# A new order of the jobs of a fused attention and MLP kernel behind its first 85 jobs, with a new table of PSUM banks

## The chip, the cores and the metric

The kernel runs on one core of a Trainium2 chip. The metric is the device time of one execution in microseconds (us); the comparison uses the median of several runs. Engine names in rows: PE is TensorE (PEld its weight loads), DVE is VectorE, ACT is ScalarE, POOL is GpSimd, SP is SyncE, which issues nearly all DMAs (SPq is its queue).

## The reference

One input of 2048 tokens by 512 features is normalised. From it two branches are computed and added to the input:

```
xn = layernorm(x)
# branch A: 32 heads of 16, four segments of 512 tokens
q, k, v = xn @ wq, xn @ wk, xn @ wv
for s in range(4):
    logits = q_s @ k_s.T * scale + mask          # causal inside the segment
    a_dot  = softmax(logits) @ v_s
    a_mem  = phi(q_s) @ M / (phi(q_s) @ z + 1e-6) # memory of the earlier segments
    o_s    = g * a_mem + (1 - g) * a_dot
    M, z   = M + phi(k_s).T @ v_s, z + sum(phi(k_s))
A = o @ wo
# branch B: MLP on layernorm(xn), 512 -> 1792 -> 512
B = gelu(layernorm(xn) @ w1 + b1) @ w2 + b2
out = x + A + B
```

## The kernel before

The work is cut into 1307 jobs, each a short run of instructions on one or more engines. Attention runs in 16 units `i` (segment times group of eight heads), the MLP in 16 half blocks `j` (256 tokens times half of the 1792 hidden features). The kernel keeps high and low halves of its numbers in f16, so that a dense product takes three matmuls for one.

Jobs are named by tuples. Those of which the texts speak:

- `T i,1` and `T i,0`: keys and queries of unit i (line 480, 12 matmuls of 512 columns); then ScalarE (514, 517) and VectorE (518, 529, 530) take the bank, and SP writes the halves to DRAM and reads them back.
- `M i,n` (621, 628): twelve score jobs that find the maximum of every row. `R i` (499, 638, 639, DMAs 641 and 644): the maxima are turned by TensorE, split by ScalarE and VectorE, written to DRAM (`md<-mhl`) and read back as two more rows of the queries (`qst<-md`).
- `S i,t,n` (661, 666, 675): the scores again, with these rows, then ScalarE's exponential and GpSimd's mask. `S i,0,0` is the first that reads the rows of `R i`.
- `pv`/`PV` (690, 698, 699, 703, 704): probabilities times values. `O i,0` to `O i,2` (714, 540, 541, 545, 546, 720, 722, 725, 726): division by the sum of the row, on all engines but TensorE.
- `Z`, `Qd`, `Q` (560, 571, 576, 577, 583): the part that reads the memory.
- `D j,f` (480 with 256 columns, 756), `G j` (763), `H j,c` (770, 771, 772): hidden features, GELU, halves; `e j,n` (797): the second MLP product, six matmuls a job.
- `out s,b` (815): the output projection of 128 tokens.

Each engine does its instructions in the order in which the jobs are recorded. Nothing but the string `ORDER` sets this: each letter takes the next job of one stream (a for the norm, f and g for `T`, i for `M` and `R`, j for `S`, k for `pv`, l for `O`, m for `Z`, `Qd`, `Q` and `K`, o for `D`, p for `G` and `H`, q for `e`, r for `out`, s for the accumulators, the rest for weights). Each PSUM tile takes the bank that the next digit of `BANKS` names, of eight (`ps0` to `ps7`); a matmul that starts a tile waits until the last reader of the bank's tile before is done. Semaphores for all waits are derived from the order.

Of the kernel before, what the change touches and what calls it, by code (L numbers as in the profile page):

```python
# [56 lines left out]
def streams():  # L57
# [42 lines left out]


ORDER = (
    "aatcucuccvavtctveecttcetcuvaactvuvtaatcattavdtubcwwvccfwxxcxwxyxyxxgyhxcoxxvwxofooowcvwzyzoiyyiazgyyziiynzoiiys"
    "ppAnziiniicvzvcniiooAzmAihiiopzqqiqcivpqjpqjijqqijizqjiqqjiiAwszBzoAskkkkmjiAojoijsoAijAqjqjasAfoAopgkkkkpjpjqq"
    "jlpoolojjjooilihAAkkkkpaiqqiqijqjqqijqjiqjqjisBfgpiiqkkkkmpliqqiooiqpBlqoBopohijjiojiijpolsjiqaqajqiqiqqiiqapka"
    "kmkktspaqijqiqjqiqajqbqajopijjgBfopkkkBkjjjlooooBlhjjjolqiqqiipkkkkjiqqijqqjjiqiqjjqiqiqiBkkkkmpliilfnplimpngrr"
    "mrjjponijqjqjinjipiskmkkmkaiijrijjoojiqsjqqjiqiiiqqkkkkihlqlfmlogojqjqjqqjjasoojmkkkkmqjiqjqjjaojjpipmooisikkkk"
    "lpilhiofmgoooqiqpppqiqiqqqiiiqqpsosmoiqqiiqiqppsslooijqjojijojijoiaakkkkmpaijqjqjaqqqjiqqjiqjqiikmkkakbqiaqqahl"
    "olfqjjojqmjgjjoolmmkkkkmhjjoojjiitjiojiippkkkkliiilnfnimpligniinipmrrijjrsijqjqiqjiqjqiipkmkkksiqjqijqjqjiqjqii"
    "qjqikmpkkkiprlqsphlfojmjgopjjlojpjoomokmkkkqiqisjojiqisjqiqijqqijqhiqqiiqjsqiiqppmkkkkilalofomqpgopaoooospmlajq"  # L110
    "qqjqqjqjqiiqiqqqjqiqqipipooooiijooppoiaakkkkmajiqpisqqjiqjqjaiqaqhjqqqjqaaqmkkkkbjlfoljqjmjgojjqolmkkkkmmjjjooj"
    "jioijoiiippkpkkkiinliifniiilnnimlgrpmjjrmjjjrrijikkpskkiqqijqiqijqqjiqjiqjqiqjiqiispqkpkskksqilqoplfojmjgjjjpoo"
    "oojolmkkkkiqjiqpsjiqiqijqjqiqijqjiqiqiqiiqqkksmkpikplolfjjqmjgjjjoooooklpkmkkjiiopjqiqijqjiqpjqiqijqiqqiqiiqikk"
    "pspkkqiplpoooopljjjqqqjqjjqooolkpskmkpkmqqqpqjpjqqqjqjqpqqjqjqqqkmkkkqlllqqqqqqqqqrrrr"
)

BANKS = (
    "012345670123457063571265407321640573216405732164053271640527163054271630542713605427105472105427105472105472015"  # L120
    "470251407251405712470512470512470536124075631254076340125637123756123576132576132576132576132576135402761350427"
    "163054273106542736574326574326537425632754632574631072456310724563071245360712453620731620731067203617621073621"
    "073621073621037621037621037261702361475023671540263701524603175246031746013746013713460713471630471630463714067"
    "314056723410523674105236741052367410527410527410527410527410527140352671450326475103264751023674523674523647253"
    "647236547236475264735264107532410765324107265431067512043675120436751204736152047361520473615270346150312750317"
    "250317253107250371257013275027135027134650132754062751340621375460376054370567403056374065374065307645307645307"
    "642153076241076241076241076253410762534621075346210754316024310264310432610432610324610324612403246013752640163"
    "754207156437120564371205647312056473120564731206547321065473265104723607423460273460273642073642073642051736420"
    "157642031765420316750316705315631705630157630157630157306173504621357462017345620147536210436024136024316403216"
    "403216403216403216740536740536740536740536271406"  # L130
)


# [777 lines left out]
```

## Time and profile before

| | |
|---|---|
| three runs | 694.29, 694.91, 697.16 us, median 694.91 |
| profiled execution | span 693.1 us; its own time beyond the span is not given |
| TensorE matmuls | 678.7 us busy, 98% of the span, 6359 instructions |
| VectorE | 535.4 us, 77% |
| ScalarE | 522.7 us, 75% |
| GpSimd | 347.2 us, 50% |
| TensorE clock | granted share 0.83 between 20 and 40 us, 1.00 in every other stretch of 20 us |

The span goes from the first to the last instruction of the program; the 1.8 us up to the median lie outside it. Matmuls overlap each other, so a TensorE that is shown busy may still have lost time between two of them: what it lost is read from the starts of its instructions and from the waits of its weight loads.

### The profile page before, as it was taken

How to read it: one execution, taken by the hardware profiler on the slowest of the kernel's cores; microseconds unless marked ns; L12 is line 12 of the kernel's file. 1: busy time of each engine (PE TensorE's matmuls, PEld its weight loads, DVE VectorE, ACT ScalarE, POOL GpSimd, SP SyncE). 2: the span in 40 equal slices, each digit the busy share in tenths (PEclk: the TensorE clock that was granted, in tenths of full speed). 3: DMA queues.
4: the chain of work that ended last, by engine and by line, in shares of the span. 5: the costliest groups of instructions: out<-in, count | busy, mean ns of one | idle time of the engine just before them, and what ended most of it. 6: DMA issues, size and time to landing. Idle time of an engine off the chain costs nothing.

```text
span 693.1 us, 16949 instructions
## 1 busy us (share of the span) xinstructions
PE 678.7 (98%) x6359; PEld 395.7 (57%) x6359; DVE 535.4 (77%) x1695; ACT 522.7 (75%) x1013; POOL 347.2 (50%) x533
## 2 busy tenths in 40 slices
PE   7799999999999999999999999999999999999997
PEld 6465556576654555566554456567564456656653
DVE  4499978897795887998798786888678595969442
ACT  5989898878795659857795697757795687778870
POOL 5276768365624425664334445454362546455752
PEclk9899999999999999999999999999999999999999
DMA  9984222420204213431113224231120416140101
GB/s 272 283 238 136 64 63 63 108 62 14 84 10 115 87 44 74 100 71 33 51 45 92 63 72 99 63 93 33 31 80 24 132 18 152 18 108 3 18 1 61
DMA packets 51790, 55.12 MB, mean 80 GB/s; under 512 B 4782, under 2 KB 40636, under 8 KB 51708
## 3 DMA queue, kind: packets, MB, share of 16 engines
q1 hardware_dynamic: 49404, 49.84, 25.3%
q0 software_dynamic: 2304, 4.20, 3.7%
q8 instruction: 50, 0.82, 0.5%
q14 instruction: 32, 0.26, 0.1%
HBM read 36.99 MB, written 17.04 MB: 78 GB/s over the span
## 4 chain that ended last, share of the span: by engine, by line
PE 78%; ACT 10%; POOL 4%; DVE 3%; issue 2%; DMA 1%; SPq 1%; POOLq 0%; ACTq 0%; DVEq 0%
PE ps L480 33%; PE ps L797 16%; PE ps L690 10%; PE ps L815 6%; PE ps L661 5%; PE ps L621 5%; ACT pt L666 2%; DVE ps L628 2%; PE ps L571 2%; PE ps L499 1%; ACT hT L763 1%; ACT hT L771 1%; SPq L252 1%; POOL w1s L371 1%; DMA pt<-in_A_wk_dram 1%
## 5 line engine op out<-in xcount | busy, mean ns | idle before, releaser
L628 DVE CUSTOM_DVE_ANT_0 ps<-ps,mask 128x512 f32<-128x512 f32 (+3 forms) x512 | 233.8, 522 | 16.1 <-PE ps L621 14.9
L666 ACT ACTIVATE pt<-ps,qkcs 128x512 f32<-128x512 f32 (+1 forms) x384 | 206.1, 624 | 35.3 <-PE ps L661 33.5
L797 PE MATMUL ps<-w2s,hT 64*128 64x512 f16 x1344 | 176.7, 376 | 0.2
L480 PE MATMUL ps<-xnT,w1s 128*128 128x256 f16 x1344 | 157.8, 273 | 0.0
L675 POOL TENSOR_SCALAR_AFFINE_SELECT pt<-pt 128x256 f32<-128x256 f32 x256 | 99.1, 414 | 92.0 <-ACT pt L666 91.0
L480 PEld LDWEIGHTS <-w1s 128*128 128x128 f16 x1344 | 127.3, 98 | 29.1 <-issue 11.3
L772 POOL TENSOR_TENSOR hT<-hh,hT 128x512 f16<-128x512 f32 x64 | 67.8, 1059 | 82.8 <-ACT hT L771 81.0
L797 PEld LDWEIGHTS <-hT 64*128 64x128 f16 x1344 | 76.3, 94 | 50.7 <-issue 6.0
L690 PE MATMUL ps<-pt,vt 128*32 128x512 f32 (+3 forms) x1024 | 77.3, 435 | 0.1
L756 DVE SCALAR_TENSOR_TENSOR hT<-ps,sc,sr 128x256 f32<-128x256 f32 x112 | 52.1, 478 | 27.2 <-PE ps L480 27.0
L628 DVE DVE_READ_ACCUMULATOR2_ANT mc<- 128x1 f32 x512 | 70.6, 138 | 0.0
L661 PE MATMUL ps<-qst,kst 50*128 50x512 f16 (+3 forms) x512 | 67.5, 298 | 0.3 <-ACT pt L666 0.2
L621 PE MATMUL ps<-kst,qst 48*128 48x256 f16 (+3 forms) x512 | 67.1, 297 | 0.5
L771 ACT ACTIVATE hT<-hh 128x512 f16<-128x512 f32 x64 | 36.6, 572 | 33.4 <-POOL hh L770 32.9
L690 PEld LDWEIGHTS ps<-pt,vt 128*32 128x32 f32 x1024 | 31.3, 109 | 42.4 <-issue 30.8
L770 POOL TENSOR_SCALAR hh<-hT,sc 128x512 f32<-128x512 f32 x64 | 41.8, 653 | 26.6 <-ACT hT L763 24.9
L720 POOL TENSOR_TENSOR nN<-nN,oT 128x512 f32<-128x512 f32 x16 | 20.3, 1267 | 61.3 <-DVE oT L546 61.3
L763 ACT ACTIVATE hT<-hT,b1t 128x256 f32<-128x256 f32 x112 | 46.4, 495 | 0.2
L480 PE MATMUL ps<-xnT,wqs 128*128 128x512 f16 x192 | 45.6, 389 | 0.0
L480 PE MATMUL ps<-xnT,wks 128*128 128x512 f16 x192 | 44.3, 379 | 0.0
L480 PE MATMUL ps<-wvs,xnT 128*128 128x512 f16 x192 | 44.0, 380 | 0.1
L815 PE MATMUL ps<-wos,oT 128*128 128x512 f16 x192 | 43.2, 380 | 0.6 <-POOL oT L726 0.6
(217 smaller groups left out, 890.0 us busy)
## 6 DMA issues: line engine op xcount, KB each, us to landing
kd<-hl SPq DMA_DIRECT2D x48, 128.0 KB
qd<-hl SPq DMA_DIRECT2D x48, 128.0 KB
kst<-kd SPq DMA_DIRECT2D x32, 192.0 KB
qst<-qd SPq DMA_DIRECT2D x32, 192.0 KB
acc<-in_A_x_dram SPq DMA_DIRECT2D x16, 256.0 KB
acc<-in_B_b_dram POOLq DMA_DIRECT2D x16, 256.0 KB, 4.1
out_dram<-acc SPq DMA_DIRECT2D x16, 256.0 KB
xt<-in_A_x_dram SPq DMA_DIRECT2D x14, 256.0 KB
```

Of the source, the lines that this page charges most:

```text
L480: T.matmul(p, wsl(ws, k, a), xsl(xs, k, b), start=s0 and i == 0, stop=s1 and i == 3 * n - 1)
L621: T.matmul(p[:, o:o + n], stk[i, 0][r, t, P * qb:P * qb + P], stk[i, 1][r, t, :n], start=True, stop=True)
L628: V.tensor_tensor_reduce(p[:, o:o + n], p[:, o:o + n], mask[:, 512 - n:], 1.0, -3e38, OP.add, OP.max, mc[:, 16 * b + 4 * t + qb:16 * b + 4 ...
L661: T.matmul(p[:, o:o + n], stk[i, 1][r, t, P * kb:P * kb + P], stk[i, 0][r, t, P * kb:], start=True, stop=True)
L666: A.activation(e[:, OFF[kbs[0]]:OFF[kbs[0]] + o], p[:, :o], AF.Exp, scale=qkcs[:, 1, i % NG:i % NG + 1])
L675: G.affine_select(v, v, pattern=[[0, 2], [1, P]], compare_op=OP.is_ge, fill=0.0, base=0, channel_multiplier=-1)
L690: T.matmul(p[32 * c:32 * c + 32, P * kb:], vt[s, kb][:, 4 * g + c, 16 * odd:16 * odd + 32], pt[i, 2 * c + odd][:, OFF[kb]:OFF[kb] + LEN[kb ...
L756: V.scalar_tensor_tensor(hz[:, fi, :], p[:, :256], col(F1 + fh), srow[hs][:, own], op0=OP.mult, op1=OP.mult)
L763: A.activation(z, z, AF.Gelu_apprx_tanh, bias=b1t[:, FH * (j % 2) + f:FH * (j % 2) + f + 1])
L772: G.tensor_tensor(hT[:, z, 1, :], t, hT[:, z, 0, :], op=OP.subtract)
L797: w = T.matmul(pes[j][a], hTs[fh][r, fi, u, P * a:P * a + P], w2s[r, fo, v, :], start=n == 0 and m == 0, stop=fi == FH - 1 and m == 2, ski ...
L815: T.matmul(p, o[:, u, P * b:P * b + P], wos[:, g, v, :], start=i == 0, stop=i == 3 * NG - 1)
```

## The change

The two strings are replaced. The first 85 letters of `ORDER` stay; behind them the same number of every letter stands in a new order, so every stream's jobs keep their order among themselves and no instruction is added or dropped. `BANKS` is a new list of the same length. The diff, cut to the first lines and the last two of each table:

```diff
 ORDER = (
-    "aatcucuccvavtctveecttcetcuvaactvuvtaatcattavdtubcwwvccfwxxcxwxyxyxxgyhxcoxxvwxofooowcvwzyzoiyyiazgyyziiynzoiiys"
+    "aatcucuccvavtctveecttcetcuvaactvuvtaatcattavdtubcwwvccfwxxcxwxyxyxxgyhxcoxxvwxofooowcswooyzyiiizvzyyzgiyvyizypz"
...
-    "pspkkqiplpoooopljjjqqqjqjjqooolkpskmkpkmqqqpqjpjqqqjqjqpqqjqjqqqkmkkkqlllqqqqqqqqqrrrr"
+    "pikkkkqiplmoooplqjjojqjjqjoolkokppkkqmqqqpjpqqqjjqqqqjpjqqjqqqqkmkkkqlqqqllqqqqqqqrrrr"
 )
 BANKS = (
-    "012345670123457063571265407321640573216405732164053271640527163054271630542713605427105472105427105472105472015"
+    "012345670123457063571265407321640266457031264537052164326705164327105264317035126473056473506437506437540463750"
...
-    "403216403216403216740536740536740536740536271406"
+    "327536427543627543672545036172450175240175264256"
 )
```

**GpSimd at `O 12,1`.** Lines 770 and 772 are `H 12` (halves of the hidden features), 720 and 722 are `O 12,1`, 675 is a mask of `S`, 780 adds the bias to an accumulator. Before:

```order
L780 DMA acc<-in_B_b_dram 128x512
L770 TENSOR_SCALAR hh<-hT_115,sc 128x512
L772 TENSOR_TENSOR hT_115<-hh,hT_115 128x2x256
L780 DMA acc<-in_B_b_dram 128x512
L770 TENSOR_SCALAR hh<-hT_115,sc 128x512
L772 TENSOR_TENSOR hT_115<-hh,hT_115 128x2x256
L720 TENSOR_TENSOR nN<-nN,oT 128x512
L722 TENSOR_TENSOR nN<-nN,ame 128x512
```

Of the change:

```order
L780 DMA acc<-in_B_b_dram 128x512
L770 TENSOR_SCALAR hh<-hT_115,sc 128x512
L772 TENSOR_TENSOR hT_115<-hh,hT_115 128x2x256
L720 TENSOR_TENSOR nN<-nN,oT 128x512
L722 TENSOR_TENSOR nN<-nN,ame 128x512
L675 AFFINE_SELECT pt<-pt 128x2x128 x2
L770 TENSOR_SCALAR hh<-hT_115,sc 128x512
L772 TENSOR_TENSOR hT_115<-hh,hT_115 128x2x256
```

One pair of `H 12` (770 and 772) moves from just ahead of `O 12,1` to behind it and behind masks.

**TensorE at `S 13,0,0`.** Line 480 with `w1s` is `D 13,1`, with `wks` `T 14,1`, with `wqs` `T 14,0`; 661 is `S 13`, 571 `Qd 13`. Before:

```order
L480 MATMUL ps6_8740<-xnT_7339,w1s_103 128x256
L661 LDWEIGHTS kst1_92
L661 MATMUL ps4_8756<-qst1_90,kst1_92 128x512
L661 LDWEIGHTS kst1_92
L661 MATMUL ps2_8757<-qst1_90,kst1_92 128x512
L571 MATMUL ps0_8762<-phq_8253,zr_8323 128x512
L571 MATMUL ps5_8763<-phq_8253,zr_8323 128x512
```

Of the change:

```order
L480 MATMUL ps6_8716<-xnT_7331,wks_100 128x512
L661 LDWEIGHTS kst1_92
L661 MATMUL ps7_8737<-qst1_90,kst1_92 128x512
L661 LDWEIGHTS kst1_92
L661 MATMUL ps2_8738<-qst1_90,kst1_92 128x512
L571 MATMUL ps0_8743<-phq_8253,zr_8707 128x512
L571 MATMUL ps4_8744<-phq_8253,zr_8707 128x512
```

`D 13,1` stood between `T 14,1` and `S 13,0,0`; it now stands behind `T 14,0`. Ahead of these rows, `e 11,12` has moved from before `R 13` to behind it.

**ScalarE between `R 7` and `S 7,0,0`.** 638 is `R 7`, 461 the norm's output of the next segment, 536 `N 7` (keys for the memory), 540 and 541 `O 6,0`, 514 and 517 `T 8,1`, 666 `S 7,0,0`. Before:

```order
L638 ACTIVATE mhl<-ps_5088 32x64
L461 ACTIVATE xnT<-ps_5098 128x4x64
L461 ACTIVATE xnT<-ps_5099 128x4x64
L461 ACTIVATE xnT<-ps_5124 128x4x64
L461 ACTIVATE xnT<-ps_5125 128x4x64
L536 ACTIVATE pkn<-ps_5139 128x4x64
L536 ACTIVATE pkn<-ps_5140 128x4x64
L540 ACTIVATE nD<-oT 128x512
L541 ACTIVATE nD<-nD 128x512
L514 ACTIVATE hl<-ps_5173 128x512
L517 ACTIVATE phk<-ps_5173,qksc 128x512
L666 ACTIVATE pt<-ps_5204,qkcs 128x512
```

Of the change:

```order
L536 ACTIVATE pkn<-ps_5127 128x4x64
L536 ACTIVATE pkn<-ps_5128 128x4x64
L638 ACTIVATE mhl<-ps_5140 32x64
L638 ACTIVATE mhl<-ps_5141 32x64
L540 ACTIVATE nD<-oT 128x512
L541 ACTIVATE nD<-nD 128x512
L514 ACTIVATE hl<-ps_5173 128x512
L517 ACTIVATE phk<-ps_5173,qksc 128x512
L666 ACTIVATE pt<-ps_5204,qkcs 128x512
L666 ACTIVATE pt<-ps_5205,qkcs 128x512
```

The norm's output and `N 7` stood between `R 7` and `S 7,0,0`, with `e 6,10` and `e 6,11` on TensorE; all of them now stand ahead of `R 7`. What is left between the two on TensorE is `D 8,0`, `T 8,1` and `e 6,12`.

## Rows read from the trace of the kernel before

**Rows 1.** Chain that ended last, shares of 80 to 560 us by line.

```profile
by line: PE ps L480 42.6%; PE ps L797 20.6%; PE ps L690 12.0%; PE ps L815 6.6%; PE ps L661 6.2%; PE ps L621 6.1%; PE ps L571 1.9%; PE ps L499 1.7%; PE ps L602 0.8%; PE ps L828 0.4%; DVE ps L628 0.4%; PE ps L343 0.3%; PE ps L427 0.2%; issue 
```

**Rows 2.** Busy us of engines (instructions) in two stretches; clock, DMA share, GB/s.

```profile
40.00:60.00 20.00, 19.97 (x138) 11.46 (x136) 19.70 (x62) 18.53 (x36) 13.29 (x14) 1.00 0.91 266
60.00:80.00 20.00, 19.52 (x203) 10.67 (x200) 19.67 (x83) 17.64 (x36) 14.07 (x20) 1.00 0.21 61
```

**Rows 3.** Groups by line: busy us, mean ns, idle before.

```profile
L546 DVE SCALAR_TENSOR_TENSOR oT<-oT,nD 128x512 f32<-128x512 f32 x16 | 14.1, 882 | 0.5
L560 DVE TENSOR_TENSOR zr<-bd,mst 64x64 f32<-64x64 f32 x48 | 12.8, 305 | 0.2
L529 DVE TENSOR_SCALAR phk<-phk,qksc 128x512 f32<-128x512 f32 x12 | 10.8, 902 | 0.0
L529 DVE TENSOR_SCALAR phq<-phq,qksc 128x512 f32<-128x512 f32 x12 | 7.2, 596 | 0.0
```

**Rows 4.** The same lines: shortest/median/longest ns, first and last start.

```profile
L529 DVE TENSOR_SCALAR phq<-phq,qksc x12: 474/478/1392, 172.2 to 616.3; 128x512 f32<-128x512 f32 x12
L546 DVE SCALAR_TENSOR_TENSOR oT<-oT,nD x16: 691/693/1669, 109.4 to 675.9; 128x512 f32<-128x512 f32 x16
L560 DVE TENSOR_TENSOR zr<-bd,mst x48: 204/219/1283, 202.3 to 655.1; 64x64 f32<-64x64 f32 x48
```

**Rows 5.** Timeline behind `T 8,1`: start us, us, instruction, [idle before <-releaser].

```profile
335.92 1.27 POOL L722 TENSOR_TENSOR nN<-nN,ame 128x512 f32<-128x512 f32 x1
335.96 1.50 DVE L529 TENSOR_SCALAR phk<-phk,qksc 128x512 f32<-128x512 f32 x1
...
338.25 0.18 PEld L571 LDWEIGHTS ps<-phq,zr 64*128 64x128 f32 x1 [0.64 <-DVE phk L530]
```

**Rows 6.** Timeline at `O 12,1` and `S 13,0,0`.

```profile
573.36 1.15 POOL L772 TENSOR_TENSOR hT<-hh,hT 128x512 f16<-128x512 f32 x1 [0.75 <-ACT hT L771]
573.39 1.67 DVE L546 SCALAR_TENSOR_TENSOR oT<-oT,nD 128x512 f32<-128x512 f32 x1
...
575.13 0.09 PEld L661 LDWEIGHTS <-kst 50*128 50x128 f16 x1 [0.21 <-DVE oT L546]
...
575.56 0.09 PEld L661 LDWEIGHTS <-kst 50*128 50x128 f16 x1 [0.34 <-DMA qst<-md]
```

**Rows 7.** Chain from `R 13` to `S 13,0,0`: start us, us, what.

```profile
569.97 0.34 DVE mhl L639 x2
...
570.33 1.40 DMA md<-mhl
...
572.06 3.46 DMA qst<-md
```

**Rows 8.** Timeline: `R 13` and `R 14` on PE, row DMAs of 14, its `S`.

```profile
569.02 0.22 PE L499 MATMUL ps<-ident,mc 64*96 64x64 f32 x2
...
604.59 0.26 PE L499 MATMUL ps<-ident,mc 64*96 64x64 f32 x2
...
606.91 0.53 SPq L644 DMA_DIRECT2D qst<-md  x2
...
609.14 0.33 PEld L661 LDWEIGHTS <-kst 50*128 50x128 f16 x6 [0.42 <-issue]
```

**Rows 9.** Timeline of the end: last `e` jobs and first `out`.

```profile
671.15 6.89 PE L797 MATMUL ps<-w2s,hT 64*128 64x512 f16 x60
...
677.97 2.61 PE L815 MATMUL ps<-wos,oT 128*128 128x512 f16 x11
...
681.20 1.04 PE L815 MATMUL ps<-wos,oT 128*128 128x512 f16 x4 [0.63 <-POOL oT L726]
```

**Rows 10.** Pieces of the chain: start us, us, what.

```profile
87.15 1.42 PE ps L480 x12
...
103.09 1.30 PE ps L797 x12
...
522.38 2.70 PE ps L480 x12
```

More of the change, by code (lines that the diff above doesn't have):

```diff
@@ L102 @@
 ORDER = (
-    "aatcucuccvavtctveecttcetcuvaactvuvtaatcattavdtubcwwvccfwxxcxwxyxyxxgyhxcoxxvwxofooowcvwzyzoiyyiazgyyziiynzoiiys"
[L104 to L112, printed above, removed]
@@ L113 @@
-    "oojolmkkkkiqjiqpsjiqiqijqjqiqijqjiqiqiqiiqqkksmkpikplolfjjqmjgjjjoooooklpkmkkjiiopjqiqijqjiqpjqiqijqiqqiqiiqikk"
-    "pspkkqiplpoooopljjjqqqjqjjqooolkpskmkpkmqqqpqjpjqqqjqjqpqqjqjqqqkmkkkqlllqqqqqqqqqrrrr"
+    "aatcucuccvavtctveecttcetcuvaactvuvtaatcattavdtubcwwvccfwxxcxwxyxyxxgyhxcoxxvwxofooowcswooyzyiiizvzyyzgiyvyizypz"
+    "nniinipiAaoiiviznmzihiioocmpqviizApjqpiqqjcqjqqiwjoizjqijqikAkziAzAskkqjioAsjioAijqjAaqsjAjfgookkAckkppjpoqjjlp"
+    "qooojjlhsooiijlkkksAkpmiqiqjiqqAjsjqqiqjiqjqBijfgqpiaBikkkkpliqqiqooihpBloqioBopjijoijijpojiaqqaqljpiqiqiqapkma"
@@ new lines @@
+    "kkktqqiqjaqiqsbiajqqijqajmoBjjigfoBkkkkpjjlolojjjoloojhqiikkpkkiqijqpiqjiqqjiqjiqBqijqiqqiqijqkkkkpiBmfnlnlganl"
+    "nmjjjrsrpijjosrjiikmkkkipjirpiijosmojjqiqjqiqjiqiikkkkhqiloplfmjgoqjqjqqjjaqjooklkmkkmijqqjjqjoijmsjpopoiikkkkl"
+    "poiilhofimqspqgooipqpqqiqsqaiiqpiqomoqiipqiqiooqpijjqoijjojijoliaakkpkkamijqjqjaqqajqsjqqijqiqiakkkkbiqaqqsmhil"
+    "lofqjjqojmjlgjjookmkkkmjjmjoohjijiotiijkkkkpliiinnliiifpmgniiplniprpmrijjrjqjiqqjiqiqjikskkkmjaiqqijqjmqjqijsqq"
+    "ijqipiskkkkpirihplqlfojmjgojjopojljookkmmkkiimqqjqpqjiiqqjisoiqjiqqjijqqqiikkpkkqhpliqpioolfqimgppoooomojqqjjqa"
@@ L115 @@
+    "qqqjliqqijqpapiqqisqiqiooopjiiopsoooaiakpkkakmijqiqjiqqjaqqaqjijqqmqjaqaskkkskhqjllbfojmjgjqjloojqmkkkkjjoojijo"
+    "jioijikpmkmkkipiifnpliiniiinlnilmgrmjjrjjjrrpiijkpkkkiqjqiqjiqjqiqijqiqjqiqijsspsqiqikkkkiplqqomlfjmjgoopomjjjj"
+    "loookkkmkiqjsipqijqijqijqpqiijqijpqqiqpiqiikskkkqiqplqslfmjjgpsjooomjjjoooklpkskkijiojqijijqijqjqiipqqiqqipqiqi"
+    "pikkkkqiplmoooplqjjojqjjqjoolokkppkkqmqqqpjpqqqjjqqqqjpjqqjqqqqkmkkkqlqqqllqqqqqqqrrrr"
 )
 BANKS = (
-    "012345670123457063571265407321640573216405732164053271640527163054271630542713605427105472105427105472105472015"
@@ L121 @@
[L121 to L129, printed above, removed]
-    "403216403216403216740536740536740536740536271406"
+    "012345670123457063571265407321640266457031264537052164326705164327105264317035126473056473506437506437540463750"
@@ new lines @@
+    "467054367075436075436074534607563476105324157620437016524370124370124370124370437120347120372410241357160245301"
+    "762453012765430127630672163071267301726306172301675401236752410372156403273402615734075327405327435027435072435"
+    "072435076243520517643205761043527061435273065147052136436710452367012367021367021372360172360172630172630176132"
+    "706213547606543217306542175306421753701523705173520173520173520651732407365127304651263570412657312635716235713"
+    "672531265736125712635107542634610275361240675312475013765271360452137460523607241356043762501340672357142357142"
@@ new lines @@
+    "315742314572431752435127453172345172316450357021407615364207215634307214320714230174213074237130427130412356704"
+    "735706047306547306457306475302614753106572413012654730126541504261502461502461524026154026105462102546171340256"
+    "371402563714650231764375024106375042165073421763504214763520275146230746230746230764230624734062736720415376452"
+    "013764523061573426301426310432631042364102613420613350427612436507124365047012536471025346723542673254673427564"
+    "327536427543627543672545036172450175240175264256"
```

## The prediction

> **What bounds the kernel now.** I read the chain that ended last first, cut to 80 to 560 us [rows 1]: the shares of its PE lines add up to 99.4% (42.6 + 20.6 + 12.0 + 6.6 + 6.2 + 6.1 + 1.9 + 1.7 + 0.8 + 0.4 + 0.3 + 0.2, with rounding). The reader is to see that for 480 us nearly every wait leads back to a matmul: 0.6%, 2.9 us, lie on another engine. A new order of the same matmuls can give back there what TensorE lost, and that is little. Then the stretches [rows 2]: between 40 and 80 us VectorE is busy 19.70 and 19.67 of each 20 us, so there it is VectorE that has no room, 0.63 us in all, and TensorE that waits for banks. Third, the lines that a VectorE instruction shares with GpSimd [rows 3, 4], and fourth the timeline at the places where such a stretched instruction reaches TensorE [rows 5, 6], where the row DMA does [rows 7, 8], and the end [rows 9]. Durations of whole jobs are pieces of the chain [rows 10]: 1.42 us for a `D` job, 0.65 for an `e` job (half of 1.30), 2.70 for a `T` or `out` job.
>
> **The change, part by part.** No instruction is added or dropped, so busy time stays and only waits move. I go through the waits in question.
>
> *VectorE waiting for GpSimd.* Undisturbed, line 529 takes 474 ns and line 546 691 [rows 4]. The groups show 10.8 + 7.2 us for 24 of line 529, 6.6 over 24 x 0.474, and 14.1 us for 16 of line 546, 3.0 over 16 x 0.691; the 48 of line 560 have a mean of 305 ns against a median of 219, 4.1 us over [rows 3, 4]. Together 13.7 us. The timeline shows what it is: line 529, issued 0.04 us after GpSimd's line 722 began, took 1.50 us [rows 5]; line 546, 0.03 us after line 772 began, took 1.67 [rows 6]. Each waited for GpSimd's instruction and then ran.
>
> The Trainium skill says this outright ("SBUF — State Buffer", section "Who interferes with whom"): a VectorE instruction in a two-port mode, or one with two inputs in SBUF against a GpSimd instruction that reads SBUF, and the GpSimd instruction hold a shared port pair in turn, and whoever comes second stands still for the whole of the other. The trace agrees at both places (1.50 and 1.67 us against 0.47 and 0.69). By that page alone one would take all 13.7 us as time to be had, 694.9 - 13.7 = 681.2 us.
>
> By the rows the sum is another: VectorE is off the chain in 99.6% of 80 to 560 us [rows 1], so its 13.7 us count only where a bank is late for TensorE. Two places show it: `Qd 7` waits 0.64 us for line 530 of `T 8,1`, behind the stretched 529 [rows 5], and `S 13,0,0` waits 0.21 us for line 546 [rows 6].
>
> At `Qd 7` the new order still puts `T 8,1`, `e 6,12`, `S 7,0`, `D 8,1` and `e 6,13` ahead of it, and both tables give its second tile bank 3, which `T 8,1` held. `O 6,1` comes one `D` job earlier (1.42 us), but the transfers of `N 7` and `R 7` ahead of it come later as well, so I see no reason why line 722 should be out of the way. I take 0; the bounds are a gain of 0.64, the whole wait, and a loss of 0.2, were 529 to meet 720 at its start as well (1.27 against 1.03 us that it lost).
>
> At `S 13,0,0` the `H 12,1` pair no longer stands in front of `O 12,1` on GpSimd, so the 0.21 us go. But the order puts something else in its place.
>
> *The rows of the maxima.* `S i,0,0` reads what `R i` sends through DRAM. For unit 13 the second read landed at 575.52 (572.06 + 3.46) [rows 7], 6.50 us after TensorE's part of `R 13` began at 569.02 [rows 8], and `S 13` waited 0.34 us for it [rows 6]. The work between them was `e`, `D`, `T`, `D`: 0.65 + 1.42 + 2.70 + 1.42 = 6.2. The order now has `e`, `e`, `D`, `T`: 0.65 + 0.65 + 1.42 + 2.70 = 5.4, 0.77 less. So the wait grows from 0.34 to about 1.1, and the 0.21 is swallowed by it: +0.55. Bounds: 0 if the read lands as fast as for unit 14, whose `S` began 4.55 us after `R` with no DMA named as releaser [rows 8]; +0.8 if the first wait stays as well. I take +0.55, since it is the same unit with the same output writes behind it.
>
> The same distance shrinks for units 5, 7 and 9 and a little for 15. Counted in the order they are `D`, `T`, `Qd` (1.42 + 2.70 + about 1 = 5.1), `D`, `T`, `e` (4.8), `e`, `T`, `D` and a transpose (5.1), and three `D` and an `e` (4.9). Bounds: 0 each by unit 14, and 1.4 + 1.7 + 1.4 + 1.6 = 6.1 together by unit 13. No output write stands next to most of them, so they are nearest to unit 14: 0, with the rest as a rival.
>
> *The end.* Behind the last `PV`, TensorE does ten `e` jobs (60 matmuls, 6.89 us) while `O 15` goes through VectorE, ScalarE and GpSimd; the first `out` job starts at 677.97, runs out of data and waits 0.63 us for line 726 [rows 9]. In the new last line of the table there are eleven `q` behind the last `k`, not ten. The extra job (0.65 us) comes from ahead of the last `pv`, so TensorE does it while it would have waited: -0.63. Nothing is queued ahead of `O 15` on the other engines that was not before. Bounds: -0.65 and 0, if ScalarE reaches `Q 15` late.
>
> *40 to 80 us.* VectorE has 0.63 us of room in 40 [rows 2], and the jobs there are the same ones. `D 0,6` now comes ahead of the scale of the second half of w1, and `M` jobs ahead of it on VectorE. I take 0, with bounds of -0.6 (its room) and +1.4 (one `D` job of TensorE in front of a wait that other engines set).
>
> *All other waits.* 2.9 us off TensorE in 80 to 560 us [rows 1], of which 0.64 is named above. An order that moves every job deals them anew. Bounds: -2.3, all gone, and +2.3, as many again. I take a gain of 1.4, above the middle because VectorE's collisions make part of them late and the POOL order shows that some were moved apart.
>
> The sum: 0 + 0.55 - 0.63 + 0 - 1.4 = -1.5 on the profiled span of 693.1, which gives 691.6; the median lies 1.8 above the span, so **693.4 us**, 0.2% less.
>
> **The rivals.**
> *Many more waits go.* All 2.9 us of the middle, the 0.63 of the end, and the 0.55 of unit 13 at the faster landing: 4.1 less, 690.8 us. For it: collisions are indeed separated at `O 12,1`. Against: `Qd 7` is not.
> *VectorE's time comes back whole.* 13.7 us, 681.2. That is what the page's lock would give if VectorE were the bound everywhere; [rows 1] speak against it with 99.4%, and only 40 to 80 us speak for it, where few of these lines start.
> *The row DMA (slower).* If units 5, 7, 9 and 15 land as late as unit 13, 6.1 us, with 0.55 for unit 13 and -0.63 at the end: 6.0 more, 700.9. It decides from a landing of about 5.0 us after `R`; for slower by 3.5 us each must take about 6. For it: unit 13's 3.46 us read. Against: unit 14.
> *The order does not do what it says.* GpSimd loses where VectorE lost: line 772 or 675 then waits, and behind it the mask for `pv`. The waits stay the size they are: 694.9.
>
> **How the numbers follow.** About 0.5%, 3.5 us, is what a measurement of this kernel can tell from no change. My forecast and the unchanged rival, both inside that bound, get 0.58 together (0.43 and 0.15); many more waits gone 0.27 and VectorE's time whole 0.02, both beyond it on the fast side; the row DMA 0.13. So faster 0.29, same 0.58, slower 0.13. The range goes from 689.5, a little beyond the fast rival, to 697.5, where half of the row DMA's price is paid; what is outside is the far end of both, about 2 in 10.
>
> **What would show it.** Right: VectorE's lines 529, 546 and 560 shorter in sum by several us and the time nearly the same; `S 13,0,0` with a wait for `qst<-md` of about 1 us; no wait for line 726 at the first `out` of the end, or under 0.1 us; `Qd 7` waiting for line 530 as before. Wrong: a chain between 80 and 560 us that leaves TensorE for more or much less than 0.6%, or weight loads of line 661 that wait for `qst<-md` in several units. The prediction fails most easily in the 1.4 us for the other waits, which no single row prices.

## The result, and the profile after

The changed kernel took 697.35 us in the median (695.43 to 700.06, 20 runs) against 695.02 for the kernel before: ratio 1.0032, 95% interval 1.0023 to 1.0041, slower by 0.3%. The profiled execution has a span of 694.9 us. The forecast was 693.4, so the time lies inside the range, but it went the wrong way.

The two stretches that answer to [rows 2], the chain from 80 to 560 us that answers to [rows 1], and the groups of [rows 3], in the profile after (columns as there):

```profile
40.00:60.00 20.00, 18.70 (x130) 11.43 (x129) 18.91 (x54) 17.02 (x33) 11.91 (x12) 1.00 0.73 209
60.00:80.00 20.00, 19.30 (x219) 11.69 (x218) 18.32 (x77) 15.94 (x31) 13.19 (x18) 1.00 0.31 94
```

```profile
by line: PE ps L480 42.6%; PE ps L797 20.6%; PE ps L690 12.0%; PE ps L815 6.6%; PE ps L661 6.4%; PE ps L621 6.1%; PE ps L571 1.7%; PE ps L499 1.6%; PE ps L602 0.7%; ACT pt L666 0.5%; PE ps L828 0.4%; PE ps L343 0.3%; PE ps L427 0.2%; ACT sr
```

```profile
L560 DVE TENSOR_TENSOR zr<-bd,mst 64x64 f32<-64x64 f32 x48 | 13.8, 326 | 0.2
L546 DVE SCALAR_TENSOR_TENSOR oT<-oT,nD 128x512 f32<-128x512 f32 x16 | 12.6, 788 | 0.5
...
L529 DVE TENSOR_SCALAR phq<-phq,qksc 128x512 f32<-128x512 f32 x12 | 6.9, 572 | 0.0
L529 DVE TENSOR_SCALAR phk<-phk,qksc 128x512 f32<-128x512 f32 x12 | 6.5, 538 | 0.0
```

The reader sees three things. The chain is on TensorE for 99.2%, as before. VectorE's three lines are stretched by 12 x (538 - 474) + 12 x (572 - 474) = 1.9, 16 x (788 - 691) = 1.6 and 48 x (326 - 219) = 5.1 us, in sum 8.6 against 13.7: 5 us were indeed taken off. And all four compute engines did less between 40 and 60 us than in [rows 2]: TensorE 1.27 us less, VectorE 0.79, ScalarE 1.51, GpSimd 1.38. Part of that is a late start of this execution (below). In a second profile of the changed kernel that has no late start (`again_after`), VectorE is as full as before (19.68 of 20 us), while TensorE (18.14) and ScalarE (17.35) still do less: they wait.

Where the time goes is read from the starts of TensorE's jobs at places that both orders have in common, in a second pair of profiles (`again_before`, `again_after`, span 693.3 and 694.2), because in the first pair the head (the 85 jobs that are the same) ends 1.4 us later in the profile after than in the one before:

| up to the start of | before | after | later by | since the row above |
|---|---|---|---|---|
| `T 1,1` (head) | 36.88 | 36.67 | -0.21 | -0.21 |
| `e 2,13` | 164.64 | 166.75 | 2.11 | **+2.32** |
| `Qd 7` | 337.66 | 339.10 | 1.44 | -0.67 |
| `T 8,0` | 339.76 | 340.28 | 0.52 | **-0.92** |
| `out 2,0` | 540.63 | 541.74 | 1.11 | +0.59 |
| `e 14,3` | 657.33 | 659.75 | 2.42 | **+1.31** |
| the end | 693.27 | 694.20 | 0.93 | **-1.49** |

This pair of executions lies 0.9 us apart, the medians of the two kernels 2.2. The rest goes with the clock. Of the changed kernel's 30 executions, 8 have a mean granted clock of 0.994 or more and a median span of 694.35 us; the other 22 lie below, with 696.0. Of 32 executions of the kernel before in the second session, 30 lie at 0.994 or more, with 693.25. A lower mean clock alone does not cost that much: over all sessions from the second on, 26 of 130 executions of the kernel before lie below 0.994, and their median span is only 0.25 us longer (693.45 against 693.2). So it must matter where in the kernel the clock is low.

### The profile page after: what moved, and what is told of

Its sections match the earlier page's. It is cut to its first block, busy times and chain, and to the rows that moved or that the text cites. A ratio compares the mean times of both kernels' runs of the same rounds, so it can differ in the third digit from the quotient of the medians.

```text
span 694.9 us, 16933 instructions
## 1 busy us (share of the span) xinstructions
PE 678.9 (98%) x6359; PEld 388.2 (56%) x6359; DVE 532.8 (77%) x1695; ACT 525.0 (76%) x1013; POOL 349.5 (50%) x533
## 4 chain that ended last, share of the span: by engine, by line
PE 92%; DVE 3%; DMA 2%; SPq 1%; ACT 1%; issue 1%; ACTq 0%; DVEq 0%
PE ps L480 39%; PE ps L797 21%; PE ps L690 10%; PE ps L815 6%; PE ps L661 6%; PE ps L621 6%; PE ps L571 2%; DVE ps L628 1%; PE ps L499 1%; DMA w1s<-in_B_w_dram 1%; SPq L252 1%; DMA pt<-in_A_wq_dram 1%; PE ps L602 1%; PE ps L343 1%; DVE zr L560 0%
## 5 line engine op out<-in xcount | busy, mean ns | idle before, releaser
L797 PE MATMUL ps<-w2s,hT 64*128 64x512 f16 x1344 | 172.8, 376 | 0.2
L797 PEld LDWEIGHTS <-hT 64*128 64x128 f16 x1344 | 70.8, 94 | 54.1 <-issue 5.1
L621 PE MATMUL ps<-kst,qst 48*128 48x512 f16 (+3 forms) x512 | 64.6, 298 | 1.3 <-DVE mc L628 0.7
L661 PE MATMUL ps<-qst,kst 50*128 50x512 f16 (+3 forms) x512 | 63.4, 297 | 0.1
```

What stands on the lines that cost most here:

```text
L621: T.matmul(p[:, o:o + n], stk[i, 0][r, t, P * qb:P * qb + P], stk[i, 1][r, t, :n], start=True, stop=True)
L661: T.matmul(p[:, o:o + n], stk[i, 1][r, t, P * kb:P * kb + P], stk[i, 0][r, t, P * kb:], start=True, stop=True)
L797: w = T.matmul(pes[j][a], hTs[fh][r, fi, u, P * a:P * a + P], w2s[r, fo, v, :], start=n == 0 and m == 0, stop=fi == FH - 1 and m == 2, ski ...
```

## The experiments

The tables were cut at places at which both orders have done the same jobs; behind a seam the bank digits are renamed so that tiles that are still held keep their banks. Jobs that the text ahead didn't need: `V s,b` (480, 593) are the values, which ScalarE copies; `wm`, `wf`, `ws` square a weight, make its scale on TensorE, ScalarE and VectorE (343, 345, 320, 321), and split it into halves (366 and 367, or 369 to 371 with GpSimd). All ratios are to the kernel before, with 95% intervals.

### Is it the head?

`again_before` and `again_after` are the two kernels again; `fill_before` and `fill_after` are both with

```diff
         for k in range(n):
+            for _ in range({"1a": (30, 8)}.get(m, (0,) * n)[k]):
+                w = ones.bitcast(F16)
+                T.matmul(p[:, 256:512], w[:, :P], w, start=True, stop=True, skip_group_check=True)
             T.matmul(p[:, :1], ones, am[:, AM[m] + k:AM[m] + k + 1], start=k == 0, stop=k == n - 1)
```

(the last line with the same `skip_group_check`). Expected:

> The kernel before, unchanged, in the same session as the next three, for the granted clock at its head in several executions. Theory A (more than half of the 2.3 us is a longer stretch at granted clock 0.5 in the 85 jobs that both kernels share): the mean clock of its executions lies at 0.993 to 0.995, and the stretch at 0.5 that begins near 25 us lasts about 6.8 us as in the profile of before. Theory B (the new waits of the order cost the 2.3 us, and the clock is no part of it): its mean clock is that of the changed kernel, 0.992, and the stretch at 0.5 lasts about 10.2 us in some profile. The time is 695.0 under both.

> The changed kernel, unchanged, again. Both theories: ratio 1.003 to the kernel before. A: where its mean clock is 0.995 its span lies near 694.2, where it is 0.992 near 695.7, and its stretch at clock 0.5 near 25 us lasts 6.8 us in the first kind and 10.2 us in the second. B: its stretch at 0.5 differs from that of before by less than 1 us, and the ratio is the same.

> The kernel before with 38 matmuls of 256 columns more, whose results nothing reads: 30 ahead of the first and 8 ahead of the second of the two matmuls that sum the squares of the first half of w1 (scale 1a). They stand where TensorE otherwise idles, waiting for ScalarE's squares at 22.6 to 25.95 and 26.5 to 27.8 us. Theory A: the stretch at 0.5 near 25 us goes or shrinks to under 3 us, and the time falls by 1 to 2.5 us from 695.0, to about 693. Theory B: the stretch may change, but the time falls by no more than it does with the changed kernel's filler, and that pair stays 2.3 us apart. If the filler itself is late for ScalarE's squares, up to 1 us is lost.

> The changed kernel with the same 38 matmuls more (results read by nothing). Theory A: both kernels now have the same head, so the difference to the kernel before with the filler falls from 2.3 to about 0.3 to 1.0 us, ratio of the two 1.0004 to 1.0014, and this kernel's time falls by 2 to 4 us, to about 694. Theory B: the difference to the kernel before with the filler stays about 2.3 us (ratio 1.003).

Measured: `again_before` 694.98 (1.0000, 0.9991 to 1.0009), `again_after` 697.09 (1.0029, 1.0019 to 1.0038). The stretch at half clock in the head lasts 6.83 us in both profiles. It is 10.24 us in the first profile of the changed kernel and also in those of `early_b`, `best` and `joined`, of which `best` and `joined` are not slower than the kernel before: it changes from execution to execution, and **theory A fell**. B is half right: 0.9 of the 2.2 us show without any difference in the head, by the table above, but the clock seems to have a part after all (below). The fillers did lift the clock (0.994 to 1.000) and brought the pair to 699.56 and 700.40 (1.0057, 1.0042 to 1.0073, and 1.0068, 1.0051 to 1.0086), 0.8 apart, but both slower: TensorE is busy 38.21 of 40 to 80 us in `fill_before`, 39.51 in `again_before`. Why a kernel with the faster head loses there was not traced, and two things changed at once, so this pair decides nothing.

### Which part of the order?

```diff
-early_old: jobs 0 to 355 of the new tables
+early_old: jobs 0 to 355 of the tables before, then the new
-early_new: jobs 356 to 1306 of the new tables
+early_new: jobs 0 to 355 of the new tables, then before
+tail_new:  before, from job 1262 (behind e 14,3) new
+mid:       before, jobs 356 to 1029 new, before, from 1262 new
```

> The first 356 jobs (to e 2,13, near 165 us) in the order of before, all behind them in the new order, with the banks of each, renamed at the seam so that tiles that are held keep theirs. Theory E (the 271 jobs behind the shared head, between 38 and 165 us, cost the loss: 1.7 us of waits at D 0,6, wf 1b, V 0,0 and others in the profile, and a lower clock in half of the executions): 694.9 - 1.4 = 693.5, since the two profiles draw 1.36 us closer behind e 2,13, and a mean clock of 0.994 to 0.995 in nearly all executions. Theory H (the lower clock comes from the shared head in the changed program, whatever order follows): about half of the executions at 0.992 or 0.990 still, 694.5 to 695.0.

> The other half: the first 356 jobs in the new order, all behind them in the order of before. Theory E: 694.9 + 1.7 + about 1 for the clock, 697 to 698, and about half of its executions at 0.992 or 0.990. Theory H: 694.9 + 1.7 = 696.6 with the clock at 0.995 in nearly all, if the place of the later jobs sets it, or the same as E, if the head does; then early_old tells.

> The order of before with the last 45 jobs (behind e 14,3) in the new order. The step of the prediction on the end says -0.63 us (one more e job behind the last PV), the two profiles draw 1.44 us closer there (3.18 to 1.74): 693.5 to 694.3, ratio 0.998 to 0.999. Rival (the wait for line 726 goes to another place): 694.9 within 0.3.

> Order of before up to e 2,13, new order to R 12, order of before to e 14,3, new order to the end, so that both stretches in which the new order lost by the profiles (38 to 165 us, +1.7; units 13 to 15, +1.0) are as before. If the differences between the two profiles add up: 694.9 - 0.9 (middle) - 1.4 (end) = 692.6, clock 0.994 to 0.995. Rival (a shifted order deals the waits anew at each seam and nothing adds up): 694.9 within 0.7.

Measured: `early_old` **693.95** (0.9984, 0.9975 to 0.9993), `early_new` **699.31** (1.0062, 1.0050 to 1.0075). Theory E held as to the place, though `early_new` lies 1.3 us above what it expected: the loss is in the jobs behind the head and ahead of `e 2,13`, and everything behind gains 1.1 us. `early_new`'s five executions all have a mean clock of 0.989 to 0.993; of `early_old`'s 11, with the same head, 9 have 0.994 or more, so theory H fell. `tail_new` 695.23 (1.0002, 0.9993 to 1.0011) is a miss; `mid` 694.21 (0.9986, 0.9977 to 0.9995) stands 1.6 us above the sum of the differences, so those do not add up.

`tail_new` tells why the end gives nothing by itself. Its waits ahead of and behind the last `PV`:

```profile
660.60 0.27 PE L661 MATMUL ps<-qst,kst 50*128 50x256 f16 x1 [0.30 <-DVE ame L577]
...
664.00 0.90 PE L661 MATMUL ps<-qst,kst 50*128 50x512 f16 x5 [0.54 <-ACT pt L666]
...
671.17 7.54 PE L797 MATMUL ps<-w2s,hT 64*128 64x512 f16 x66
678.64 10.53 PE L815 MATMUL ps<-wos,oT 128*128 128x512 f16 x48
```

and its busy time there (columns as in [rows 2]: TensorE, its loads, VectorE, ScalarE, GpSimd):

```profile
650.00:660.00 10.00, 10.00 (x101) 5.95 (x101) 3.44 (x9) 9.89 (x19) 7.10 (x13) 1.00 0.16 29
660.00:670.00 10.00, 9.12 (x86) 5.88 (x86) 1.96 (x3) 9.81 (x18) 7.08 (x13) 1.00 0.01 2
```

The 0.63 us of [rows 9] are gone from the start of `out`, but the `e` job that fills them was taken from ahead of `PV`, where TensorE now waits 0.30 + 0.54 us (in the kernel before it is busy all of 660 to 670 us). ScalarE is busy 9.89 and 9.81 of 10 us in both kernels. That speaks for ScalarE setting the pace there, so that TensorE's `e` jobs only choose where the wait shows; no run with less work on ScalarE tested it.

### What inside 38 to 165 us?

In the changed kernel, TensorE, VectorE and GpSimd between 43 and 54 us (`again_after`; start us, us, engine, instruction):

```profile
45.98 0.86 DVE L756 SCALAR_TENSOR_TENSOR hT<-ps,sc,sr 128x256 f32<-128x256 f32 x2
...
46.65 1.16 POOL L371 TENSOR_TENSOR wks<-pt,wks 128x512 f16<-128x512 f32 x1 [1.80 <-ACT wks L370]
...
46.76 1.59 DVE L367 SCALAR_TENSOR_TENSOR w2s<-w2s,sc 128x512 f16<-128x512 f32 x1
...
46.89 0.72 PE L621 MATMUL ps<-kst,qst 48*128 48x512 f16 x8 [0.91 <-DVE hT L756]
47.54 2.76 PE L480 MATMUL ps<-xnT,wqs 128*128 128x512 f16 x12
50.24 0.55 PE L621 MATMUL ps<-kst,qst 48*128 48x512 f16 x3
51.00 0.37 PE L621 MATMUL ps<-kst,qst 48*128 48x384 f16 x3 [0.22 <-DVE mc L628]
52.11 1.02 PE L343 MATMUL ps<-am,ones 128*128 128x1 f32 x8 [0.73 <-DVE mc L628]
52.99 0.36 PE L345 MATMUL ps<-am,ones 128*128 128x1 f32 x2
53.22 2.97 PE L480 MATMUL ps<-wvs,xnT 128*128 128x512 f16 x13
```

The three waits sum to 1.86 us. Three suspects are seen at once: the bank table (`M 0,0` takes the bank that `D 0,6` took right ahead of it, so it waits for 756), the order (`D 0,6` ahead, and `V 0,0`, which asks nothing of VectorE, behind `wf 1b`), and a new collision (367 takes 1.59 us, 0.74 when alone, against GpSimd's 371). The experiments, with one that moves `D 0,6` alone and its control (`before_lru`):

```diff
 after_lru: the new order; banks of jobs 86 to 128 dealt anew, longest handed out first
 after_w1:  ... M 0,3
+           V 0,0
            ... M 0,4   wf 1b
+           D 0,6
 after_qk2: ... wl 2b 0
+           ws QK 2
            A 0,0   ws v 3   D 0,5   D 0,6   ws 2a 0   wm 1b 0   ...   wm 1b 1
-           ws QK 2
 d06_new (from the kernel before):
            D 0,5
+           D 0,6
            M 0,0 ... wf 1b
-           D 0,6
            M 0,4
 before_lru: the order before; banks of jobs 86 to 128 dealt by the rule of after_lru
```

(In `after_w1` the two jobs leave their places ahead of `ws 2a 0` and `V 0,1`. The bank rule of `after_lru` holds in all five.)

> The changed kernel in its own order; only the bank digits of jobs 86 to 128 are dealt anew, each tile in the bank that was handed out longest ago (behind them the digits are renamed so that held tiles keep their banks). In the changed kernel M 0,0 takes the bank that D 0,6 had taken right ahead of it, and TensorE waits 0.91 us there for VectorE's line 756. Theory K (the bank table makes the early loss): that wait goes, and with it TensorE's idle time between 45 and 55 us (1.9 us) and the lower clock in half of the executions: 695.0 to 695.8. Theory V (the order makes it: VectorE is busy all of 45 to 55 us, D 0,6 and a stretched line 367 stand ahead of M 0,0 in its queue, and V 0,0, which needs no VectorE, comes too late to cover it): the wait moves to the next banks, M 0,3 to wf 1b, and the time stays 697.1 within 0.5.

> The changed kernel with two jobs put back: V 0,0 (2.76 us of TensorE, nothing for VectorE) behind M 0,3 and ahead of wf 1b, and D 0,6 behind wf 1b, as the kernel before has them; banks of jobs 86 to 128 dealt by the same rule as in after_lru. Theory V: TensorE idles less than 0.5 us between 45 and 55 us, the clock does not fall near 53 us, 694.2 to 695.3, more than 0.7 us below after_lru. Theory K: the same time as after_lru within 0.4 us.

> The kernel before with the one job D 0,6 moved to its new place, ahead of M 0,0; banks of the jobs around it dealt by the same rule, so that M 0,0 does not get the bank of D 0,6. Theory V (order): VectorE is 0.47 us later for M 0,0 and TensorE loses 0.4 to 1.5 us, 695.3 to 696.4. Theory K (bank): 694.9 within 0.4.

> The kernel before in its own order, with the banks of jobs 86 to 128 dealt by the rule that d06_new and after_w1 use (longest handed out first): the control for both. If the moved job D 0,6 made d06_new 1.25 us slower: 694.9 within 0.4. If the bank rule did: 696.2.

> The changed kernel with one weight job put back: ws QK 2 (GpSimd's and ScalarE's split of a piece of wk) ahead of A 0,0 and so ahead of ws 2a 0, as before; banks of jobs 85 to 128 dealt as in after_lru. In the changed kernel GpSimd's line 371 of it (46.65, 1.16 us) meets VectorE's line 367 of ws 2a 1, which takes 1.59 us instead of 0.74. If a collision between VectorE and GpSimd is paid in full where VectorE has no room (45 to 55 us): line 367 takes 0.74 there, 697.1 - 0.85 = 696.2 against 697.3 of after_lru. If it is not paid: 697.2 within 0.4.

Measured:

- `after_lru` 697.31 (1.0032, 1.0020 to 1.0045), no change: **theory K fell**. The wait at `M 0,0` is gone, and one of 0.94 us for 628 stands at `M 0,3` in its place.
- `d06_new` 696.16 (1.0020, 1.0011 to 1.0029), and its control `before_lru` 694.78 (0.9998, 0.9989 to 1.0007): one moved job costs **1.3 us**, as theory V expected.
- `after_w1` 696.22 (1.0018, 1.0010 to 1.0027), 1.1 below `after_lru`, but short of the 694.2 to 695.3 that V expected. TensorE is filled again up to 55 us, and 8 of 11 executions keep a clock of 0.994 or more; between 60 and 70 us it is busy only 8.83 of 10. So these two jobs are not all of it.
- `after_qk2` 697.39 (1.0032, 1.0021 to 1.0043), no change against `after_lru`. The collision is gone, as the second row below shows (367 takes 0.75 us), but VectorE waits 0.79 us for ScalarE ahead of the same instruction:

```profile
46.14 0.86 DVE L756 SCALAR_TENSOR_TENSOR hT<-ps,sc,sr 128x256 f32<-128x256 f32 x2
47.79 0.75 DVE L367 SCALAR_TENSOR_TENSOR w2s<-w2s,sc 128x512 f16<-128x512 f32 x1 [0.79 <-ACT w2s L366]
```

How `D 0,6` costs it: ScalarE in the trace of before, and below it ScalarE and TensorE in `d06_new`.

```profile
52.48 0.25 ACT L320 ACTIVATE fa<-ps,sc 128x2 f32<-128x2 f32 x1
...
54.79 2.91 ACT L763 ACTIVATE hT<-hT,b1t 128x256 f32<-128x256 f32 x7
...
59.59 0.57 ACT L593 ACTIVATE vt<-ps 128x512 f32<-128x512 f32 x1
```

```profile
53.05 0.26 ACT L320 ACTIVATE fa<-ps,sc 128x2 f32<-128x2 f32 x1 [0.41 <-PE ps L345]
...
55.38 2.90 ACT L763 ACTIVATE hT<-hT,b1t 128x256 f32<-128x256 f32 x7
...
60.18 0.57 ACT L593 ACTIVATE vt<-ps 128x512 f32<-128x512 f32 x1
...
60.80 0.39 PE L621 MATMUL ps<-kst,qst 48*128 48x512 f16 x2 [1.20 <-ACT vt L593]
```

`D 0,6` is 1.3 us of TensorE ahead of `wf 1b`. ScalarE waits 0.41 us for that scale; behind it in its queue stand the GELU (763) and the copy of the values (593), all 0.6 us later; the bank that 593 frees is late, and TensorE, which has `D 0,6` behind it by then, stands for 1.20 us. In this trace TensorE is 0.7 us later than in the kernel before when it reaches `R 0` (67.46 against 66.75), and stays late to the end; its execution, 695.45 us, was the fastest of `d06_new`, so the trace shows the way of the loss but only part of the 1.3 us.

`early_a` and `early_b` cut once more, at about 62 us:

```diff
+early_a: the 129 jobs that before has done by M 0,11, in its order; all others in the new order
+early_b: the 129 jobs that the new order has done by K 0, in its order; all others as before
```

> The new order, but the 129 jobs that the kernel before has done by M 0,11 (about 62 us) stand first, in the order of before; all others follow in the new order. Banks of jobs 85 to 153 dealt anew, longest handed out first, without those that e and pv hold. Theory V1 (the early loss lies between 38 and 62 us, at D 0,6 and V 0,0): 694.0 to 695.0, and TensorE idle under 0.5 us between 45 and 60 us. Theory V2 (half of it lies between 62 and 165 us, in how the new order goes on, as after_w1 still stood 2.2 us above early_old): 695.5 to 696.5.

> The complement: the 129 jobs that the changed kernel has done by K 0 stand first, in the new order, all others follow in the order of before. Banks of jobs 85 to 133 dealt as in early_a. Theory V1: 697.0 to 699.5, as early_new (699.3). Theory V2: 696.0 to 697.2, about half of the loss of early_new.

Measured: `early_a` **694.03** (0.9987, 0.9978 to 0.9996), as fast as `early_old`; `early_b` 698.33 (1.0048, 1.0035 to 1.0062). **V1 held**: the loss, about 3 us, lies in some 44 jobs behind the head, between 38 and 62 us. The banks dealt anew are no rival for it, as `after_lru` and `before_lru` changed nothing.

The clock, in `early_new` and then in `again_before` (columns as in [rows 2]; the granted clock stands ahead of the DMA share):

```profile
46.00:53.00 7.00, 5.13 (x35) 2.50 (x33) 7.00 (x22) 4.99 (x13) 4.70 (x5) 1.00 0.67 242
53.00:56.40 3.40, 3.40 (x12) 1.75 (x12) 3.40 (x7) 2.93 (x6) 2.57 (x3) 0.50 0.66 189
```

```profile
46.00:53.00 7.00, 7.00 (x44) 4.02 (x43) 7.00 (x24) 6.13 (x15) 5.47 (x6) 1.00 0.88 318
53.00:56.40 3.40, 3.40 (x23) 1.65 (x22) 3.30 (x12) 3.37 (x7) 1.57 (x2) 1.00 0.67 196
```

After 7 us with 1.87 us of idle time in three pieces, the longest 0.92, the clock stands at half (1.2 instead of 2.4 GHz) for 3.4 us. What that costs is seen on the 24 matmuls of `V` that begin near 53 us: 5.34 us in `early_b`, 7.03 in `after_lru` and `after_qk2`, 1.7 us more. Such a stretch, somewhere between 53 and 57.8 us, stands in the profiles of `early_new`, `after_lru`, `after_qk2` and `fill_after`, all with the new order there, and in none of a kernel that has the order before there. It is missing in both profiles of the changed kernel and in that of `early_b`. The idle time alone does not decide it: `again_after` has the same three waits, 1.86 us, and keeps its full clock.

### The gain behind it

```diff
+m7:     before, jobs 537 to 675 new (S 5,3,0 to Qd 7)
+best:   before, jobs 356 to 675 new
+joined: before, jobs 356 to 730 new (to R 8)
```

> The order of before with jobs 537 to 675 (from S 5,3,0 to Qd 7, 276 to 338 us) in the new order. The prediction took 0 for Qd 7, with a gain of 0.64 as its bound. The two profiles say that the new order keeps line 529 of T 8,1 clear of GpSimd there (0.48 us against 1.50) and that TensorE is 0.93 us less late at T 8,0. If that is what it gives alone: 693.7 to 694.2 and no wait for line 530 at Qd 7. If the gain is given back behind it: 694.9 within 0.3.

> The order of before with jobs 356 to 675 (165 to 338 us) in the new order, the only long stretch in which the traces of early_old and m7 draw ahead of before and keep it. By early_old's starts (+0.16 at e 2,13, -1.40 at T 8,0): 694.9 - 1.5 = 693.4, below m7's 694.2 and both kernels. If the part ahead of job 537 gives nothing: 694.2, as m7.

> As best, but with the seam at R 8 (377 us) and not at S 7,2,0 (338 us), so that S 7,2,0 and T 8,0 keep the banks of the new table. In best's trace S 7,2,0 waits 0.26 us for line 756 at the seam and TensorE gains 0.29 us there, where early_old gains 0.92. If the bank at the seam kept back the rest of the gain: 694.45 - 0.6 = 693.85, or up to 693.5 by early_old's starts at R 8 (-1.34 behind e 2,13); no kernel here is faster then. If not: 694.4.

Measured: `m7` 694.18 (0.9986, 0.9977 to 0.9995) as expected; `best` 694.45 (0.9992, 0.9983 to 1.0001), a miss by 1 us; `joined` 694.25 (0.9990, 0.9981 to 0.9998), short of 693.85. The place `Qd 7` in the profile of the changed kernel, which answers to [rows 5]:

```profile
338.41 0.48 DVE L529 TENSOR_SCALAR phk<-phk,qksc 128x512 f32<-128x512 f32 x1
338.49 1.53 POOL L722 TENSOR_TENSOR nN<-nN,ame 128x512 f32<-128x512 f32 x1
...
339.87 1.02 PE L571 MATMUL ps<-phq,zr 64*128 64x512 f32 x4
```

Line 529 begins 0.08 us ahead of 722 and not 0.04 behind it. It takes 0.48 us, 722 pays (1.53 against 1.27 in [rows 5]), and `Qd 7` waits for nothing. In `best` a new wait at the seam keeps part of the gain back:

```profile
338.61 0.37 PE L661 MATMUL ps<-qst,kst 50*128 50x512 f16 x1 [0.26 <-DVE hT L756]
```

In `joined` that wait is gone and TensorE gains 0.93 us there, but 0.5 of it is lost again between `R 8` and `pv 11,0,0`. The weight loads name the place, `S 8`, which waits for the rows of `R 8`:

```profile
382.61 0.33 PEld L661 LDWEIGHTS <-kst 50*128 50x128 f16 x5 [0.59 <-DMA qst<-md]
```

From `R 8` to the `out` job behind `S 8,0,0` TensorE takes 6.72 us (376.44 to 383.16), against 6.24 for the same jobs in `again_before`, in which no DMA is named there. The wait does not come from the order alone: `before_lru`, with the order of before, has one of 0.30 us at the same place, and `early_old` one of 0.26.

The versions `early_old`, `early_a`, `m7` and `mid` are 0.13 to 0.16% faster than the kernel before, and so faster than the changed one; their intervals do not tell them apart.

## Why the prediction was wrong

**40 to 80 us: the step that failed.** It said "I take 0, with bounds of -0.6 and +1.4 (one `D` job of TensorE in front of a wait that other engines set)". The mechanism in the bracket is what happened: that one job costs 1.3 us by itself (`d06_new` against `before_lru`). The whole loss between 38 and 62 us is 697.1 - 694.0 = 3.1 us (`again_after` against `early_a`), with the other moves there, among them `V 0,0` behind `wf 1b`, and perhaps the half clock that follows TensorE's idle time in some executions. Zero was the wrong choice in a stretch for which [rows 2] showed 0.63 us of room on VectorE, 0.51 on TensorE and 3.8 on ScalarE in 40: with so little room, a job that is moved ahead of another engine's input makes that engine late, and little is left to make it up. The upper bound had the price of one such job and neither a second nor the clock. This step decides the result: without the stretch the new order gains 1.1 us (`early_old`), not far from the forecast's 1.5.

**VectorE waiting for GpSimd.** Right in the main: 5 us fewer on the three lines, and the only gain that was traced to them is at `Qd 7`, one of the two places that the prediction named. The Trainium skill ("SBUF — State Buffer", section "Who interferes with whom") has whoever comes second stand still; [rows 5] and the rows of 338.41 and 338.49 us above show both orders of arrival. In both, less was lost than the rest of the other instruction: 1.03 us of 1.23 by line 529, 0.26 of 0.40 by line 722. What that is worth in time the rows decide: 0.85 us of it in a stretch where VectorE has no room came back as 0.79 us of waiting for ScalarE (`after_qk2`).

**`Qd 7`.** Wrong, on the other side: 0 was taken, and 0.92 us was gained in the second pair of profiles, more than the bound of 0.64: the weight load's wait of 0.64 us held TensorE up for longer than itself. `m7`, in which only jobs 537 to 675 have the new order, gains 0.7. The jobs ahead of it were read correctly, but which of 529 and 722 comes first was settled by 0.1 us, and no table of the order shows that.

**`S 13,0,0` and the row DMA.** Wrong, +0.55 expected. In the profile after, which answers to [rows 6 to 8], no DMA is named:

```profile
570.53 0.26 PE L499 MATMUL ps<-ident,mc 64*96 64x64 f32 x2
...
576.02 0.10 PEld L661 LDWEIGHTS <-kst 50*128 50x128 f16 x2 [0.42 <-issue]
```

The distance from `R 13` to the first weight load of `S 13` did shrink about as worked out, from 6.11 (569.02 to 575.13) to 5.49 us. What failed is the landing time, which was taken from one profile and is not the same in the next. From `R 13` to `T 14,0` the kernel before takes 7.95 us in the profile of [rows 6 to 8] and 7.51 in `again_before`, where `S 13` waits for no DMA; the changed kernel takes 6.90 in `after` and 7.11 in `again_after`, where the read is named. So the wait is 0 or 0.4 us under the old order and 0 or 0.2 under the new one, and one profile could not price it. The slower rival built on it is not what made the kernel slower: of the units that it names, only 15 shows a wait for the read, 0.15 us in `after`.

**The end.** The wait was read correctly, but not what its removal is worth: TensorE no longer waits for 726 at the first `out` (a weight load waits 0.28 us in `after`), and `tail_new` shows the time spent in advance, in front of `PV`, with no gain in all (1.0002). In the whole change the stretch gains 1.49 us, after units 13 to 15 have lost 1.31 ahead of it. `mid`, in which units 13 to 15 have the old order ahead of the new end, takes 35.95 us from `e 14,3` to its end, against 35.94 in `again_before` and 34.45 in `again_after`: without the loss there is no gain. That ScalarE sets this is likely, and not shown.

**All other waits**, -1.4 expected. Behind the early stretch the order gives 1.1 us (`early_old`), most of it at `Qd 7` (0.92 in `early_old`'s own profile), which the prediction had taken out of this term; what the other waits give was not measured by itself. That the sum behind 80 us comes near the forecast is luck: a guess of -1.4 stands where a gain at `Qd 7` was, and +0.55 and -0.63 that were not there nearly cancel.

What stays open is which jobs beside `D 0,6` and `V 0,0` make up the rest of the early loss (`after_w1` still stands 2.2 us above `early_a`), whether the slower executions of the changed kernel have the half clock near 53 us (their mean clock speaks for it, neither of its profiles shows it), and why the row DMA lands later in one execution than in another.

## What to carry to other kernels

A new order is priced stretch by stretch, and first where several engines have no room at once: there a job that is moved ahead of a scale, a GELU or a copy delays whoever waits for them. In the one case that was measured alone, the price was about the job's own duration (1.3 us), not zero. Time that two engines lose on each other was worth something only where TensorE waited for it (0.9 us at one place, of 13.7 in all). A wait that comes and goes between two profiles of one kernel, as that for the row DMA, has no price in a single trace. To find where an order lost, cut both orders at the places where their job sets agree and join the halves: here two such kernels (`early_old` and `early_new`) told more than either trace.

## What was not expected of the hardware

In `early_new` the granted clock fell to half at 53 us, after 7 us in which TensorE never idled for more than 0.92 us at a time (5.13 of 7 us busy); with the same idle time in `again_after` it did not fall. In the head, with the same 85 jobs, the half clock lasted 6.83 us in most profiles and 10.24 in four; the two profiles of the changed kernel are 1.3 us apart at `T 1,1`, with 10.24 and 6.83 us, which is more than half of the change under study. The row DMA of one unit landed in time in one execution of a kernel and 0.4 us late in another. Of two instructions on VectorE and GpSimd, 0.08 us decided which of them was stretched.
